# Where two small VectorE instructions of the third batch's routing stand in the queue (clustered attention and mixture of experts on one core)

## The chip, the core and the metric

The kernel runs on one core of one Trainium2 chip, as one program. The metric is the device time of the program in microseconds. Before the change it is 662.63 us, the median of three runs (661.48 to 662.72).

## What is computed

Four batches of 768 tokens with 8 heads of width 64 go through an attention in which a query sees only the keys of its own cluster (the nearest of 16 centroids). The result, 3072 rows of 512, goes through a layer of experts: a row whose skip score is positive is sent to the best of 8 experts, and the expert's answer, times a gate, is added to the row.

```
q_assign = argmax(q_n . c_n);  k_assign = argmax(k_n . c_n)
scores = q k^T / 8, kept where q_assign == k_assign
x = softmax(scores) v                       # 3072 x 512
do_compute = x @ w_skip > 0
e = argmax(x @ w_gate);  g = softmax(x @ w_gate)[e]
out = x;  out[do_compute] += g * (relu(x @ w1[e]) @ w2[e])
```

## The kernel before

**Attention.** Two heads make a pair; four batches of four pairs give 16 pairs, numbered 0 to 15. Each pair is worked in 24 score steps (`NS`). A score step is two matmuls into a PSUM bank `ps` (L604, L605), the exponential on ScalarE into one of twelve slots of `PT` (L607), and an add into a running sum `acc` on GpSimd (L613 for the first add of a half pair, L619 for the others; ten adds to a half pair, and steps 0 and 1 of each half have none). Six steps at a time are multiplied with the values (L630). Beside them run, for the next pair, the 24 maxima: a matmul into a bank (L569) and a row maximum of it into `M` on VectorE (L571). Seven PSUM banks go round among all these; a bank is taken by a matmul again when the instruction that reads it has finished.

**Routing.** When a batch's four pairs are done, its tokens are routed while the next batch's attention runs. `route_slots` (L828) does the second half: each token's rank in its expert's list, one-hots of rank and half, the matmuls that write the lists into `slotacc`, and at its end `route_e` (L983), which keeps for each token a code for the overflow lists. `route_e` begins with `cc` (L989), the product of the token's expert one-hots `ohd` (bf16) and the experts' codes `ecode` (float32), 128x48 with both inputs in SBUF, and `c` (L992), its sum over the experts. Five more small instructions (L995 to L1003) make the code of them.

**The early list.** Behind the third batch (the routing that starts with pair 11, `self.npair - HP - 1`) the list of expert 0 is made ready early: `early_lists` (L1149) counts (L1153), pads (L1156 to L1159), makes the list's row numbers (`slot_ids`, L1195 to L1198) on VectorE, and GpSimd gathers the rows `xe` with an indirect DMA (L1181). The rows are turned by TensorE later (L1172).

**What sets the order.** The order of the attention's instructions is written out by hand: every task has a due time in score steps, counted from its pair's start, and `steps` (L304) takes the tasks in the order of these times and records their instructions. Each engine runs its own in that order. A task that is a generator hands back a pair `(t,)`: go on when the clock stands at `t`. For `route_slots` these times stand in the tuple `SLOTS` (L57): of its 20 entries the last seven are those of `route_e`, 91.67 for `cc`, 91.68 for `c`, and 97.66 to 97.7 for the rest. For the early list the times are 85.4 for the count, 85.67 for padding and row numbers, and 0.2 later for the gather. Counted from pair 11 both lie in pair 14. At 85.8 stands the rest of an expert weight's split on VectorE, `rawW` (L1024).

Of the kernel before, what the change touches and what calls it, by code (L numbers as in the profile page):

```python
# [25 lines left out]
HP = H // 2  # L26
# [29 lines left out]
         53.16, 53.17, 53.18, 61.67, 61.68, 67.67, 67.68, 73.66, 73.67)  # L56
SLOTS = (59.1, 59.11, 59.12, 59.13, 73.7, 73.71, 77.16, 77.17, 77.18, 77.19, 79.66, 82.9, 83.1,  # L57
         91.67, 91.68, 97.66, 97.67, 97.68, 97.69, 97.7)
FIRST = {
    0: {  # L60
        "load_v": -18.9, "sims": -20.0, "hi": (-19.9, -19.8, -19.7, -19.6), "assign": (-19.0, 0.1, 0.01, 0.01, 0.01, 0.01),
# [18 lines left out]
class Kernel:  # L80
# [246 lines left out]
    def tasks(self, i):  # L327

        p, last = {**PLAN, **FIRST.get(i, {})}, i == self.npair - 1
        r = [(s, lambda s=s: self.score(i, s)) for s in range(NS)]  # L330
# [497 lines left out]

    def route_slots(self, i, bt):

        wait = iter([(t,) for t in SLOTS])
        yield from self.route_c(i, bt * KT, KT, wait)
        yield next(wait)
        yield from self.route_cum(KT, wait)
        yield next(wait)
        yield from self.route_d(i, bt * KT, KT, wait=wait)
        yield next(wait)
        yield from self.route_e(i, bt * KT, KT, wait)
# [657 lines left out]
```

## Time and profile before

| | before |
|---|---|
| time, median of 3 runs | 662.63 us (661.48 to 662.72) |
| time of the profiled execution | 662.12 us |
| its span, first to last instruction | 660.4 us |
| TensorE busy | 639.8 us, 97% |
| VectorE busy | 505.6 us, 77% |
| ScalarE busy | 417.3 us, 63% |
| GpSimd busy | 359.9 us, 54% |
| mean granted TensorE clock | 0.989 |

The profile is of one execution. The span leaves out 1.7 us of that execution's own time, at its two ends. PE is TensorE, DVE VectorE, ACT ScalarE and POOL GpSimd; times are counted from the first instruction. A busy share is of the span; "L989" is line 989 of the kernel before. The clock is a share of TensorE's full 2.4 GHz, so 0.50 is its lower level, 1.2 GHz. In the timeline instructions of one kind in a row are put together as "x8", with the first one's start and the time to the last one's end; consecutive instructions of one engine overlap a little in it. In brackets stands the idle time before, and what ended it.

### The profile page before, as it was taken

What the parts mean: (1) busy time and instruction counts of PE and PEld (TensorE: products, weight loads), DVE (VectorE), ACT (ScalarE), POOL (GpSimd) and SP (SyncE); (2) the same over time, 40 slices, a digit from 0 to 9 for tenths busy, and PEclk for the clock granted to TensorE, in tenths of its full rate; (3) what the DMA queues carried; (4) which work ended last, traced back from release to release, by engine and by line L of the source; (5) the groups of instructions that cost most, each with busy time, mean ns of one, the idle gap of its engine ahead of it and who ended that gap; (6) DMA issues with size and microseconds to landing.
All of it is one profiled execution on the core that took longest, in us unless ns stands there. A gap on an engine that the chain in (4) does not pass through costs nothing.

```text
span 660.4 us, 12489 instructions
## 1 busy us (share of the span) xinstructions
PE 639.8 (97%) x4019; PEld 475.9 (72%) x4019; DVE 505.6 (77%) x1031; ACT 417.3 (63%) x935; POOL 359.9 (54%) x384
## 2 busy tenths in 40 slices
PE   7899999999999999999999999799999999999994
PEld 3667776776767767767767767455798898899893
DVE  7877787688988869998769899786689867666721
ACT  7467778677777777767777778454365454544620
POOL 8876777857758867668677777440331321121101
PEclk9899999999999999999999999799999999999998
DMA  7388647866786466555754652140386758566620
GB/s 216 108 198 223 157 140 197 224 184 171 200 224 175 124 168 163 165 137 158 202 145 119 156 136 82 45 151 25 128 283 222 258 189 276 184 199 226 200 77 33
DMA packets 54323, 110.12 MB, mean 167 GB/s; under 512 B 8599, under 2 KB 22807, under 8 KB 54256
## 3 DMA queue, kind: packets, MB, share of 16 engines
q1 hardware_dynamic: 51232, 101.92, 53.7%
q0 software_dynamic: 2624, 7.18, 3.1%
q8 instruction: 33, 0.54, 0.3%
q14 instruction: 34, 0.28, 0.2%
q10 hardware_dynamic: 400, 0.20, 0.1%
HBM read 60.93 MB, written 10.55 MB: 108 GB/s over the span
## 4 chain that ended last, share of the span: by engine, by line
PE 79%; DVE 8%; issue 6%; DMA 5%; ACT 0%; POOL 0%; POOLq 0%; DVEq 0%
PE ps L630 20%; PE ps L604 11%; PE ps L569 10%; PE ps L605 9%; DMA out<-yo,idw 3%; DVE M L571 3%; PE ph L1030 3%; PE ph L1029 3%; PE ph L1028 3%; PE py L1029 2%; PE py L1028 2%; PE py L1030 2%; PE ps L729 2%; PE ps L586 2%; PE ps L480 2%
## 5 line engine op out<-in xcount | busy, mean ns | idle before, releaser
L619 POOL TENSOR_TENSOR acc<-acc,PT 128x384 f32<-128x384 f32 x246 | 241.6, 1010 | 56.5 <-ACT PT L607 56.1
L607 ACT ACTIVATE PT<-ps 128x384 f32<-128x384 f32 x384 | 184.2, 492 | 94.7 <-PE ps L605 77.8
L571 DVE TENSOR_REDUCE M<-ps 128x1 f32<-128x384 f32 x384 | 200.3, 553 | 47.5 <-PE ps L569 46.5
L630 PE MATMUL ps<-PT,vt 128*64 128x385 f32 x768 | 140.2, 500 | 0.1
L604 PE MATMUL ps<-D 98*128 98x384 f32 x384 | 135.5, 353 | 4.1 <-DVE M L571 3.5
L569 PE MATMUL ps<-D 96*128 96x384 f32 x384 | 135.6, 359 | 0.8 <-ACT D L549 0.7
L605 PE MATMUL ps<-D 128*128 128x384 f32 x384 | 131.0, 341 | 0.0
L630 PEld LDWEIGHTS ps<-PT,vt 128*64 128x64 f32 x768 | 49.8, 137 | 57.8 <-issue 52.9
L604 PEld LDWEIGHTS ps<-D 98*128 98x128 f32 x384 | 73.4, 191 | 24.9 <-issue 19.0
L613 POOL TENSOR_TENSOR acc<-PT 128x384 f32<-128x384 f32 x64 | 54.3, 868 | 67.7 <-ACT PT L607 36.1
L569 PEld LDWEIGHTS ps<-D 96*128 96x128 f32 x384 | 73.7, 193 | 20.4 <-ACT x L751 7.2
L1186 POOL DMA_INDIRECT out<-yo,idw x15 | 20.3, 1350 | 114.0 <-DVE yo L1062 103.8
L605 PEld LDWEIGHTS ps<-D 128*128 128x128 f32 x384 | 73.6, 192 | 0.0
L1314 ACT ACTIVATE hh<-ph 128x256 fp32r<-128x256 f32 x56 | 21.4, 383 | 46.4 <-PE ph L1030 46.4
L1315 DVE SCALAR_TENSOR_TENSOR hl<-ph,hh 128x256 fp32r<-128x256 f32 x56 | 23.6, 422 | 33.6 <-ACT hh L1314 33.4
L1286 ACT ACTIVATE D<-wraw 128x1024 fp32r<-128x1024 f32 (+1 forms) x45 | 44.1, 1002 | 6.2 <-PE py L1030 4.7
L1028 PE MATMUL ph<-x2l,D 128*128 128x256 f32 x168 | 47.7, 284 | 0.0
L1029 PE MATMUL ph<-x2h,D 128*128 128x256 f32 x168 | 47.6, 283 | 0.0
L1028 PE MATMUL py<-D,hh 128*128 128x512 f32 x112 | 45.0, 402 | 0.0
L751 ACT ACTIVATE x<-ps,rs 128x64 f32<-128x64 f32 x162 | 36.1, 322 | 10.1 <-DVE rs L683 9.1
L1287 DVE TENSOR_TENSOR D<-wraw,D 128x1024 fp32r<-128x1024 f32 (+1 forms) x29 | 34.3, 1183 | 6.2 <-ACT D L1286 5.4
L431 DVE TENSOR_TENSOR raw<-raw,D 128x768 fp32r<-128x768 f32 x28 | 38.3, 1367 | 0.0
(311 smaller groups left out, 1068.9 us busy)
## 6 DMA issues: line engine op xcount, KB each, us to landing
wraw<-w SPq DMA_DIRECT2D x72, 512.0 KB, 4.9
D<-D SPq DMA_DIRECT2D x124, 192.0 KB, 3.4
raw<-qk SPq DMA_DIRECT2D x16, 768.0 KB, 5.6
D<-raw SPq DMA_DIRECT2D x60, 192.0 KB, 4.1
vt<-v SPq DMA_DIRECT2D x16, 384.0 KB, 4.4
out<-x SPq DMA_DIRECT2D x31, 192.0 KB, 3.3
D<-mk SPq DMA_DIRECT2D x120, 24.0 KB, 1.9
out<-yo,idw POOLq DMA_INDIRECT x15, 4.5
```

Source lines behind the costliest of these rows:

```text
L431: eng.tensor_tensor(out=lo.bitcast(F32R), in0=lo, in1=c[f"hi{t}"].bitcast(F32), op=ALU.subtract)
L569: nc.tensor.matmul(sm, lhsT=c["qm"][a][0:96, j * P:(j + 1) * P], rhs=c["kb"][a][0:96, hf * HALF:(hf + 1) * HALF], start=True, stop=True)
L571: nc.vector.tensor_reduce(out=c["m"][:, j, a, hf:hf + 1], in_=sm, axis=AX.X, op=ALU.max)
L604: nc.tensor.matmul(ps, lhsT=c["kb"][a][0:98, ks], rhs=c["qm"][a][0:98, sl], start=True, stop=False)
L605: nc.tensor.matmul(ps, lhsT=c["kc"][a][:, ks], rhs=c["qc"][a][:, sl], start=False, stop=True)
L607: nc.scalar.activation(out=pt, in_=ps, func=AF.Exp, scale=D ** -0.5)
L613: nc.gpsimd.tensor_tensor(out=acc, in0=self.pt(i, s - 2)[:, :HALF], in1=pt, op=ALU.add)
L619: (nc.vector if dve else nc.gpsimd).tensor_tensor(out=acc, in0=acc, in1=pt, op=ALU.add)
L630: nc.tensor.matmul(av[a * D:(a + 1) * D, :], lhsT=c["vt"][:, kt, a * D:(a + 1) * D], rhs=self.pt(i, hf * 2 * KT + kt * 2 + a), start=(kt = ...
L1028: mm(ps, lhsT=ah, rhs=bl, start=first, stop=False)
L1029: mm(ps, lhsT=ah, rhs=bh, start=False, stop=False)
L1286: nc.scalar.activation(out=h[:, cs], in_=r[:, cs], func=AF.Copy)
```

## The change

In the third batch's routing alone, the times of `cc` and `c` become 85.9 and 85.91, in place of 91.67 and 91.68. All else, and the other batches, stay. The changed kernel has two lines more, so its line numbers behind L57 are higher by one, and behind L829 by two.

```diff
+CODES = {91.67: 85.9, 91.68: 85.91}
...
     def route_slots(self, i, bt):
 
-        wait = iter([(t,) for t in SLOTS])
+        early = i == self.npair - HP - 1
+        wait = iter([(CODES.get(t, t) if early else t,) for t in SLOTS])
         yield from self.route_c(i, bt * KT, KT, wait)
```

The order of TensorE, ScalarE, GpSimd and the DMA queues is the same in both kernels; one place on VectorE differs. VectorE before, in pair 14 behind the row numbers of the early list (`ps_81` and the like are the PSUM banks, `M_200` the maxima, `MX_195` their maximum over a half):

```order
L1024 TENSOR_TENSOR rawW<-wraw,D 128x1024
L571 TENSOR_REDUCE M_200<-ps_81 128x1
L571 TENSOR_REDUCE M_200<-ps_87 128x1
L578 TENSOR_REDUCE MX_195<-M_200 128x3x2
L571 TENSOR_REDUCE M_200<-ps_86 128x1
L571 TENSOR_REDUCE M_200<-ps_82 128x1
L571 TENSOR_REDUCE M_200<-ps_84 128x1
L571 TENSOR_REDUCE M_200<-ps_83 128x1
L571 TENSOR_REDUCE M_200<-ps_85 128x1
L989 TENSOR_TENSOR cc<-ohd,ecode 128x48
L992 TENSOR_REDUCE c_4571<-cc 128x6
L571 TENSOR_REDUCE M_200<-ps_84 128x1
```

Here `cc` and `c` stand behind seven maxima. VectorE in the changed kernel, the same stretch:

```order
L1026 TENSOR_TENSOR rawW<-wraw,D 128x1024
L572 TENSOR_REDUCE M_200<-ps_81 128x1
L991 TENSOR_TENSOR cc<-ohd,ecode 128x48
L994 TENSOR_REDUCE c_4517<-cc 128x6
L572 TENSOR_REDUCE M_200<-ps_87 128x1
L579 TENSOR_REDUCE MX_195<-M_200 128x3x2
L572 TENSOR_REDUCE M_200<-ps_86 128x1
L572 TENSOR_REDUCE M_200<-ps_82 128x1
L572 TENSOR_REDUCE M_200<-ps_84 128x1
L572 TENSOR_REDUCE M_200<-ps_83 128x1
L572 TENSOR_REDUCE M_200<-ps_85 128x1
L572 TENSOR_REDUCE M_200<-ps_84 128x1
```

The two have moved up past six maxima and `MX_195`, and stand behind the first maximum that follows `rawW`. TensorE beside it, from the matmul that fills bank `ps_87` for the second of these maxima to the one that takes the bank again:

```order
L569 MATMUL ps_87<-D 128x384
L604 MATMUL ps_83<-D 128x384
L605 MATMUL ps_83<-D 128x384
L569 MATMUL ps_86<-D 128x384
L604 MATMUL ps_85<-D 128x384
L605 MATMUL ps_85<-D 128x384
L569 MATMUL ps_82<-D 128x384
L604 MATMUL ps_81<-D 128x384
L605 MATMUL ps_81<-D 128x384
L569 MATMUL ps_84<-D 128x384
L604 MATMUL ps_87<-D 128x384
```

Nothing has moved on TensorE: nine matmuls stand between the two uses of `ps_87`, in both kernels.

## Rows read from the trace of the kernel before

**Rows 1.** The page's first line.
```profile
span 660.4 us, 12489 instructions
```

**Rows 2.** TensorE's waits, whole span: waiter, releaser, us in total, times, longest.
```profile
PE ps L604 <- DVE M L571: 3.5, 1, 3.5
```

**Rows 3.** Busy time of each engine in stretches of 4 us, with TensorE's granted clock.
```profile
410.00:414.00 4.00, 4.00 (x25) 2.52 (x23) 4.00 (x3) 3.00 (x8) 4.00 (x6) 1.00 0.18 68
414.00:418.00 4.00, 0.63 (x4) 0.31 (x2) 3.97 (x4) 0.98 (x2) 3.30 (x4) 0.98 0.00 0
418.00:422.00 4.00, 3.88 (x13) 2.96 (x15) 3.56 (x13) 2.30 (x4) 0.00 (x0) 0.50 0.00 0
422.00:426.00 4.00, 4.00 (x16) 1.84 (x13) 1.25 (x2) 1.05 (x4) 0.00 (x0) 0.67 0.59 180
```

**Rows 4.** TensorE's timeline, 408 to 425 us: start, length, instruction, idle before and releaser.
```profile
408.67 0.34 PE L604 MATMUL ps<-D 98*128 98x384 f32 x1
...
409.74 0.49 PE L586 MATMUL ps<-ident,MX 128*128 128x128 f32 x3
410.16 2.16 PE L630 MATMUL ps<-PT,vt 128*64 128x385 f32 x12
412.25 0.44 PE L604 MATMUL ps<-D 98*128 98x384 f32 x1
...
418.12 0.69 PE L604 MATMUL ps<-D 98*128 98x384 f32 x1 [3.49 <-DVE M L571]
...
420.21 0.84 PE L729 MATMUL ps<-ident,oT 128*128 128x128 f32 x3
420.98 3.95 PE L630 MATMUL ps<-PT,vt 128*64 128x385 f32 x12
424.86 0.44 PE L604 MATMUL ps<-D 98*128 98x384 f32 x1
```

**Rows 5.** VectorE's timeline, 407 to 418 us.
```profile
407.75 0.55 DVE L571 TENSOR_REDUCE M<-ps 128x1 f32<-128x384 f32 x1
...
408.29 2.40 DVE L571 TENSOR_REDUCE M<-ps 128x1 f32<-128x384 f32 x5
410.61 6.75 DVE L989 TENSOR_TENSOR cc<-ohd,ecode 128x48 f32<-128x48 bf16 x1
417.40 0.20 DVE L992 TENSOR_REDUCE c<-cc 128x6 f32<-128x48 f32 x1
```

**Rows 6.** GpSimd's timeline, 407 to 424 us.
```profile
407.08 1.38 POOL L1181 DMA_INDIRECT xe<-out,idre  x1 [1.43 <-issue]
408.49 1.68 POOL L613 TENSOR_TENSOR acc<-PT 128x384 f32<-128x384 f32 x2
410.13 7.16 POOL L619 TENSOR_TENSOR acc<-acc,PT 128x384 f32<-128x384 f32 x8
```

**Rows 7.** All `cc` (ns: min/median/max), then the first batch's, and GpSimd beside it.
```profile
L989 DVE TENSOR_TENSOR cc<-ohd,ecode x5: 176/867/6753, 202.1 to 475.9; 128x48 f32<-128x48 bf16 x3, 128x24 f32<-128x24 bf16 x2
...
202.08 0.87 DVE L989 TENSOR_TENSOR cc<-ohd,ecode 128x48 f32<-128x48 bf16 x1
...
199.51 7.92 POOL L619 TENSOR_TENSOR acc<-acc,PT 128x384 f32<-128x384 f32 x8
```

**Rows 8.** Weight splits of the expert stage: group (busy us, mean ns), then one beside a gather.
```profile
L1287 DVE TENSOR_TENSOR D<-wraw,D 128x1024 fp32r<-128x1024 f32 x27 | 32.9, 1220 | 6.2 <-ACT D L1286 5.4
...
515.01 1.22 DVE L1287 TENSOR_TENSOR D<-wraw,vtW 128x1024 fp32r<-128x1024 f32 x1
...
514.43 1.21 POOL L1181 DMA_INDIRECT xg<-out,idr  x1 [0.31 <-PE ph L1030]
```

**Rows 9.** ScalarE's timeline, 407 to 410 us.
```profile
407.16 2.09 ACT L607 ACTIVATE PT<-ps 128x384 f32<-128x384 f32 x4 [0.45 <-ACT rawW L1022]
```

**Rows 10.** The early gather's issue and landing (us); the turn of its rows on TensorE.
```profile
xe<-out,idre POOLq DMA_INDIRECT x1, 4.7
...
426.02 0.60 PE L1172 MATMUL ps<-ident,xe 128*128 128x128 f32 x4
```

## The prediction

> **What bounds the kernel now.** First the page: TensorE is busy 97% of the 660.4 us span [rows 1], so only time that TensorE loses can be won. Then TensorE's waits: the longest by far is one single wait, 3.5 us before a score matmul (L604), ended by a row maximum on VectorE (L571) [rows 2]. Then the stretches around it: from 410 to 414 us TensorE is busy throughout at full clock, from 414 to 418 it works 0.63 us of 4, and then the granted clock is 0.50 for 4 us and 0.67 over the next 4, that is, at the lower level for most of this time [rows 3]. So the wait is paid twice, as idleness and as slow work behind it.
>
> Then the three engines in that window. TensorE idles 3.49 us up to 418.12 [rows 4]. VectorE shows why: it isn't idle, it stands in one instruction, `cc`, from 410.61 for 6.75 us, with the maxima that TensorE's banks wait for queued behind it [rows 5]. GpSimd runs eight adds (L619) without a gap from 410.13 for 7.16 us, to 417.29; `cc` ends 0.07 us later, at 417.36 [rows 5, 6]. The five `cc` take 0.176 us at the least, 0.867 in the middle and 6.753 at the most, and the 0.87 us one also lies in a run of adds, but waited for no more than one add's length (7.92 us for eight is 0.99 each) [rows 7]. I read the 6.75 us as a small VectorE instruction with two SBUF inputs kept out by GpSimd's adds, and here by all that were left of the run, not by one.
>
> What the long hold has of its own isn't plain from the rows. It came into the run with GpSimd late: the gather's wait and the gather (407.08 to 408.46) had put the adds behind, so ten of them followed without a pause [rows 6]. For the forecast it is enough that the hold ended with the run.
>
> **The change, part by part.** No instruction is added or removed; two move on VectorE, no other queue changes.
>
> Removed, the idleness: 3.49 us on TensorE [rows 4]. Its cause is gone from the old place: behind the seventh maximum VectorE goes straight on to the next one.
>
> Removed, the slow work: from 418.12 to 424.86, 6.74 us, TensorE does six score and maximum matmuls, three turns (L729) and twelve L630 [rows 4]. The same kinds at full clock stand just before: six such matmuls from 408.67 to 409.74, 1.07 us; three turns of the same 128x128 size (L586) to 410.16, 0.42; twelve L630 to 412.25, 2.09 [rows 4]. Together 3.58, so 6.74 - 3.58 = 3.16 us come back. By the granted clock it would be 4 x 0.50 + 4 x 0.33 + 4 x 0.02 = 3.4 us [rows 3]; I take 3.16, since it is counted on the very instructions, and keep 3.4 as an end. Sum removed: 6.65 us.
>
> Added at the new place: `cc` would start where the second maximum started, at 407.75 [rows 5]. An unhindered `cc` of 128x48 isn't in the trace; the shortest, half the size, took 0.176 us, so I estimate 0.2, and `c` took 0.20 [rows 5, 7]. The second maximum (bank `ps_87`) then starts 0.4 later and ends at 407.75 + 0.40 + 0.55 = 408.70. TensorE takes that bank again with the L604 at 408.67 [rows 4], so it waits some 0.1 us with the signal's way. The banks behind it keep the same distance, so this is paid once. Ends: 0 and 0.40 us; a gain is excluded, as the maxima only get later. I take 0.1, since 408.70 is next to 408.67. Cover for the rest is VectorE's own slack: no further maximum is due until the L604 at 412.25 and its follower have run [rows 4].
>
> Is `cc` free at 407.75? GpSimd then is in the gather, 0.67 us after its start, and the first add comes at 408.49 [rows 6]: 0.74 us for 0.2 us of work. Beside a gather the trace has a nearer row than any add: a weight split (L1287, two SBUF inputs) that began at 515.01, inside the gather of 514.43 to 515.64, took 1.22 us, which is the mean of its 27 (1220 ns) [rows 8]. So a gather that runs doesn't hold up such an instruction, and I take no wait. The other end is to wait out the gather or more, which are rivals below.
>
> The Trainium skill (SBUF — State Buffer, "Who interferes with whom") says that a VectorE instruction with two SBUF inputs contends with a GpSimd instruction that reads SBUF, and that the second to issue is blocked until the first finishes. On the adds the trace agrees that there is a block, but not on its length: by the rule the hold would have ended with the add under way, at about 411.1 instead of 417.3, and there would have been nothing to win here. Where rule and row differ the row decides.
>
> What is late next: the other small instructions of the code (L995 to L1003) and the next weight split stay behind six more maxima. At full clock these would be over about 416, so their first can still meet the run of adds, which ends at 417.29 [rows 6], and lose up to 1.3 us. No maximum of pair 14 is left behind them, so TensorE doesn't wait for that. The gathered rows land 4.7 us after issue, about 413.2, and are turned at 426.02, in future some 6.6 us earlier, 419.4 [rows 10]: 6 us to spare.
>
> Sum: 662.12 - 3.49 - 3.16 + 0.10 = 655.57; I say **655.5 us**. The profiled execution lies 0.5 us under the median of its three runs (662.63), which is within their scatter.
>
> **The rivals.**
>
> *The gather does block `cc`.* If the gather, which started first, keeps `cc` out until it ends at 408.46, `cc` is 0.71 us later than 407.75 [rows 5, 6]; if it then gets in before the add, the second maximum ends at 409.41, TensorE loses 0.8 us in place of 0.1, and the time is 656.2. Against it speaks the split that ran freely beside a gather [rows 8]. This is the case if `cc` lasts longer than about 0.5 us. The rule of the Trainium skill named above (SBUF — State Buffer, "Who interferes with whom") would make it so, since the gather reads its row numbers from SBUF and was issued first.
>
> *`cc` is held at the new place, by gather and adds* (the slower one). If `cc` hasn't begun when the add starts at 408.49, it waits as before until GpSimd runs dry. TensorE would then stop at 408.67 for want of `ps_87`; by then ScalarE has made four slots of `PT` to add (to 409.25) [rows 9], so GpSimd has four adds: 1.68 us from 408.49, and two of 7.16 / 8 = 0.90, to 411.9 [rows 6]. `cc` ends at 412.0, `c` and the maximum at 412.75, and TensorE idles about 3.95 us, 0.45 more than now. The same work follows at low clock: 662.6. If a second stretch like that of 6.74 us fell to the low level, 3.4 us more: 666.0. The idleness is only an eighth longer than now, so I take a quarter of that way, 663.5. For it: the 6.75 us itself [rows 5]. Against: the 0.74 us that are free of adds [rows 6], and the split beside a gather [rows 8].
>
> *Something later takes part back.* What follows moves forward by 6.6 us, but weight loads and gathers of the expert stage take their time from landings. For it: DMA queues stand still while TensorE does (share 0.00 from 414 to 422 [rows 3]), so the stall may have given them a lead. Against: 6 us to spare at the gather, and TensorE full at 422 to 426. It would cost 1.5 to 5.5 us: 657 to 661.
>
> *No change.* The hold isn't GpSimd's doing, and `cc` or its follower waits the same elsewhere: 662.1. For it: one add was enough in the other batch. Against: the end 0.07 us behind the run's.
>
> **How the numbers follow.** Forecast as reasoned 0.77; gather blocks 0.06; part taken back 0.05; no change 0.06; held at the new place 0.06. The first three are faster by over 0.2% (1.3 us, about what a measurement of this kernel can tell from no change): 0.88. The fourth, and a sixth of the last, whose lower end is within 0.2%, are the same: 0.07. The rest of the last is slower: 0.05. The range starts at 654.5: 662.12 less 3.49 and 3.4, with nothing added, is 655.2, and the shortest of the runs (661.48) lies 0.6 below the profiled one. It ends at 659.0, with the second case and half of the third in it; what is left out above is some 0.15.
>
> **What would show it.** In the new profile `cc` should stand between 407.7 and 408.2, lasting 0.2 us, right behind one maximum and during the gather. GpSimd's ten adds should be as before, to about 417.3, and TensorE should have no wait of over 0.5 us between 406 and 425, at clock 1.00. The turn of `xe` should come at about 419.4, and all behind it 6.5 us earlier than before. It would be wrong if `cc` lasts over 0.5 us (the gather blocks), if VectorE stands in it till about 412 and TensorE idles from 408.8 (held), if another VectorE instruction shows several us in that run of adds, or if the wait is gone and the span isn't shorter by 6 us, when the new waits of the expert stage would name what took it.

## The result, and the profile after

The changed kernel takes **654.36 us** (median of 6 runs, 654.25 to 655.62); the kernel before, run beside it, 661.92 (6 runs, 659.60 to 662.72). The ratio is 0.9897, its 95% interval 0.9876 to 0.9917: 1.0% faster. The forecast was 655.5, in a range from 654.5 to 659.0, so the measured median lies 0.14 us below the range's lower end. The profiled execution took 654.36 us as well.

TensorE's waits in the whole span of the changed kernel (waiter, releaser, us in total, times, longest):

```profile
span 652.6 us, 12489 instructions
...
PE ps L587 <- DVE MX L579: 1.6, 3, 1.2
PE ps L278 <- DVE ones_bf L131: 1.2, 1, 1.2
```

The row of [rows 2], one wait of 3.5 us for a maximum, is gone; what now stands first stood second before. The stretches of [rows 3] in the changed kernel (TensorE's busy time comes first, its granted clock third from the end):

```profile
410.00:414.00 4.00, 4.00 (x24) 3.11 (x21) 1.99 (x4) 2.82 (x6) 3.98 (x5) 1.00 0.00 0
414.00:418.00 4.00, 4.00 (x25) 2.48 (x24) 4.00 (x10) 3.24 (x5) 2.15 (x3) 1.00 0.11 33
418.00:422.00 4.00, 4.00 (x32) 2.01 (x31) 2.77 (x6) 3.19 (x9) 2.64 (x3) 1.00 0.45 154
422.00:426.00 4.00, 4.00 (x26) 2.47 (x25) 3.13 (x7) 2.78 (x6) 0.86 (x1) 1.00 0.29 65
```

TensorE is busy in all 16 us and the clock stays at its upper level, where it stood at 0.50 and 0.67 behind the wait. TensorE's timeline of the changed kernel, for [rows 4]:

```profile
407.28 0.33 PE L570 MATMUL ps<-D 96*128 96x384 f32 x1
407.48 0.44 PE L605 MATMUL ps<-D 98*128 98x384 f32 x1
...
409.08 2.16 PE L631 MATMUL ps<-PT,vt 128*64 128x385 f32 x12
411.18 0.44 PE L605 MATMUL ps<-D 98*128 98x384 f32 x1
...
414.88 2.16 PE L631 MATMUL ps<-PT,vt 128*64 128x385 f32 x12
416.97 0.44 PE L605 MATMUL ps<-D 98*128 98x384 f32 x1
...
418.15 0.60 PE L1174 MATMUL ps<-ident,xe 128*128 128x128 f32 x4
```

From the L604/L605 at 412.25 (now 411.18) to the one at 424.86 (now 416.97) it was 12.61 us and is 5.79. VectorE's timeline of the changed kernel, for [rows 5]:

```profile
406.06 0.55 DVE L572 TENSOR_REDUCE M<-ps 128x1 f32<-128x384 f32 x1
406.53 0.20 DVE L991 TENSOR_TENSOR cc<-ohd,ecode 128x48 f32<-128x48 bf16 x1
406.76 0.20 DVE L994 TENSOR_REDUCE c<-cc 128x6 f32<-128x48 f32 x1
406.88 0.55 DVE L572 TENSOR_REDUCE M<-ps 128x1 f32<-128x384 f32 x1
...
415.13 1.05 DVE L997 CAST ri<-rank 128x6 int32<-128x6 f32 x1
```

GpSimd's timeline of the changed kernel, for [rows 6]:

```profile
405.83 1.40 POOL L1183 DMA_INDIRECT xe<-out,idre  x1 [1.41 <-issue]
407.27 1.68 POOL L614 TENSOR_TENSOR acc<-PT 128x384 f32<-128x384 f32 x2
408.91 7.24 POOL L620 TENSOR_TENSOR acc<-acc,PT 128x384 f32<-128x384 f32 x8
```

`cc` takes 0.20 us beside the gather and ends 0.54 us before the first add starts. The adds are as they were; what meets them now is the small `ri`, which takes 1.05 us, to the last add's end, with nobody waiting for it. All five `cc`, for [rows 7], in ns:

```profile
L991 DVE TENSOR_TENSOR cc<-ohd,ecode x5: 175/198/865, 200.9 to 467.9; 128x48 f32<-128x48 bf16 x3, 128x24 f32<-128x24 bf16 x2
```

The 6.75 us is gone, and the first batch's, held for one add, is now the longest.

Not all of the difference is the change's. The gather starts 1.25 us earlier than before, although nothing ahead of it has moved. The stretches from 20 us on show where that comes from, first in the kernel before:

```profile
20.00:24.00 4.00, 3.46 (x15) 2.88 (x16) 3.81 (x8) 2.88 (x6) 3.86 (x6) 0.73 0.18 69
24.00:28.00 4.00, 4.00 (x23) 3.13 (x23) 2.77 (x6) 2.21 (x5) 3.23 (x4) 0.84 0.13 31
```

and in the changed kernel:

```profile
20.00:24.00 4.00, 3.23 (x20) 2.78 (x19) 3.90 (x8) 3.24 (x7) 3.86 (x6) 1.00 0.19 75
24.00:28.00 4.00, 4.00 (x26) 2.57 (x27) 3.67 (x9) 2.62 (x6) 4.00 (x5) 1.00 0.13 31
```

The execution profiled before had 0.73 and 0.84 of the clock there, the one after 1.00. From 33 us on up to the gather the same maxima start about 1.2 us earlier than before, and that lead stays the same on the way. The clock there goes by the execution, not by the kernel: of the first four variants below, three show 1.00 from 20 to 24 us and one 0.74.

### The profile page after: what moved, and what is told of

Same layout as the page of the kernel before. It is cut to its first block, busy times and chain, and to the rows that moved or that the text cites. A ratio compares the mean times of both kernels' runs of the same rounds, so it can differ in the third digit from the quotient of the medians.

```text
span 652.6 us, 12489 instructions
## 1 busy us (share of the span) xinstructions
PE 635.6 (97%) x4019; PEld 473.0 (72%) x4019; DVE 499.6 (77%) x1031; ACT 417.8 (64%) x935; POOL 360.0 (55%) x384
## 3 DMA queue, kind: packets, MB, share of 16 engines
q0 software_dynamic: 2624, 7.18, 3.2%
## 4 chain that ended last, share of the span: by engine, by line
PE 80%; DVE 7%; issue 6%; DMA 5%; ACT 0%; POOL 0%; POOLq 0%; DVEq 0%
PE ps L631 20%; PE ps L605 11%; PE ps L570 11%; PE ps L606 10%; DMA out<-yo,idw 3%; PE ph L1031 3%; PE ph L1030 3%; PE ph L1032 3%; DVE M L572 3%; PE py L1031 2%; PE py L1030 2%; PE py L1032 2%; PE ps L730 2%; PE ps L587 2%; PE ps L481 2%
## 5 line engine op out<-in xcount | busy, mean ns | idle before, releaser
L631 PE MATMUL ps<-PT,vt 128*64 128x385 f32 x768 | 138.4, 495 | 0.1
L605 PE MATMUL ps<-D 98*128 98x384 f32 x384 | 134.6, 350 | 0.6 <-ACT D L592 0.6
L631 PEld LDWEIGHTS ps<-PT,vt 128*64 128x64 f32 x768 | 49.4, 136 | 56.8 <-issue 52.2
L605 PEld LDWEIGHTS ps<-D 98*128 98x128 f32 x384 | 72.8, 190 | 21.0 <-issue 18.6
```

Of the source, the lines that this page charges most:

```text
L605: nc.tensor.matmul(ps, lhsT=c["kb"][a][0:98, ks], rhs=c["qm"][a][0:98, sl], start=True, stop=False)
L631: nc.tensor.matmul(av[a * D:(a + 1) * D, :], lhsT=c["vt"][:, kt, a * D:(a + 1) * D], rhs=self.pt(i, hf * 2 * KT + kt * 2 + a), start=(kt = ...
```

## The experiments

The forecast rested on a hold whose length it could not explain: GpSimd's adds kept `cc` out for all that were left of the run, while the first batch's `cc` waited for one [rows 7]. So the experiments ask what makes a hold long. Medians of the kernel before, run beside the variants: 660.42 us (13 runs) for the first four, 660.88 (7) for the next four, 661.45 (3) for the three after these, 660.61 (7) for the last.

**A memset among the adds.** The kernel before with

```diff
+        tasks.append((14 * NS + 18.5, 0, self.gap))
...
+    def gap(self):
+        self.nc.gpsimd.memset(self.fix.tile([P, D], F32, name="gap"), 0.0)
```

> The kernel before (cc at its old place), with one small GpSimd instruction more: a fill of a 128x64 tile, which reads nothing, between the fifth and the sixth of the ten adds. Theory (cc is kept out by adds that follow each other without a pause): the fill is the pause, so cc begins at its old place, but ends when the fifth add does, after some 2.2 us in place of 6.75; VectorE goes on before TensorE is out of banks, TensorE has no long wait, and the time is that of the changed kernel, about 6.5 us under the one before. Rival (the hold has another cause, or ends only when TensorE and GpSimd are out of work): 6.7 us as before, and the time of before.

Measured 661.25 us, ratio 1.0007 (0.9994 to 1.0021). VectorE's and GpSimd's timelines of this variant:

```profile
409.43 6.85 DVE L990 TENSOR_TENSOR cc<-ohd,ecode 128x48 f32<-128x48 bf16 x1
...
408.95 2.64 POOL L620 TENSOR_TENSOR acc<-acc,PT 128x384 f32<-128x384 f32 x3
411.54 0.14 POOL L1151 MEMSET gap<- 128x64 f32 x1
411.65 4.56 POOL L620 TENSOR_TENSOR acc<-acc,PT 128x384 f32<-128x384 f32 x5
```

`cc` stands past the memset and ends at 416.28, 0.07 us behind the last add. The theory's 2.2 us didn't come: an instruction that only writes, 0.14 us of it, does not let VectorE in. It is shorter than `cc` itself (0.20 us); a longer one in this place was not tried.

**The gather later.** The kernel before with the gather behind the eighth add instead of ahead of the first:

```diff
-        yield 0.2
-        self.gather(self.xe[:, 0, :], rd, self.ntok - S)
         yield (91.66,)
         self.early = wr, self.slot_gates(acc, const, P, 1, "e")
+        yield (93.5,)
+        self.gather(self.xe[:, 0, :], rd, self.ntok - S)
```

> The kernel before (cc at its old place), with the early gather later by 7.6 score steps, between the eighth and ninth of the ten adds; GpSimd is then not late when the adds begin. Theory (the long hold needs a GpSimd that is behind with its adds): cc still falls into the run of adds, but waits for one add, at most 1.0 us, and the time is 5 to 6.5 us under that of before; the rows land later, which may cost TensorE up to 1 us at their turn. Rival (an instruction with two SBUF inputs that comes into any run of adds by itself is kept out to the end of the run): 5 us or more, and the time of before.

Measured 655.26 us, ratio 0.9916 (0.9891 to 0.9940), with `cc` at its old place: it stands from 409.45 for 0.64 us, one add's rest. So the place alone isn't it; something that comes with the gather ahead of the adds is. This run takes away two things at once, the gather and the lateness of the adds.

**A probe at the old place.** The changed kernel with an instruction of `cc`'s form where `cc` stood:

```diff
+        tasks.append((11 * NS + 91.67, 0, self.probe))
...
+    def probe(self):
+        if not hasattr(self, "prb"):
+            self.prb = self.fix.tile([P, KT, E], F32, name="prb")
+        self.nc.vector.tensor_tensor(out=self.prb, in0=self.ident_bf[:, :KT * E].rearrange("p (j e) -> p j e", e=E),
+                                     in1=self.ecode.unsqueeze(1).to_broadcast([P, KT, E]), op=ALU.mult)
```

> The changed kernel, with an instruction of cc's form (128x48, one bf16 and one float32 input, both in SBUF, no one waits for its result) at cc's old place. Theory (the place decides): it is held for about 6.7 us there, TensorE idles about 3.5 us, and the time is back at that of before. Rival (it was cc's own data or neighbours): 0.2 to 1.0 us, and the time of the changed kernel.

Measured 655.87 us, ratio 0.9922 (0.9895 to 0.9950). Its timelines, VectorE's two rows and then GpSimd's:

```profile
407.72 0.90 DVE L992 TENSOR_TENSOR cc<-ohd,ecode 128x48 f32<-128x48 bf16 x1
...
411.64 2.17 DVE L1155 TENSOR_TENSOR prb<-ident_bf,ecode 128x48 f32<-128x48 bf16 x1
...
407.19 1.24 POOL L1190 DMA_INDIRECT xe<-out,idre  x1 [1.58 <-issue]
...
410.13 3.61 POOL L621 TENSOR_TENSOR acc<-acc,PT 128x384 f32<-128x384 f32 x4
414.42 3.61 POOL L621 TENSOR_TENSOR acc<-acc,PT 128x384 f32<-128x384 f32 x4 [0.68 <-ACT PT L609]
```

The probe is held over the ends of adds, up to 413.74, where GpSimd runs out of `PT`, and ends 0.07 us later: here the run pauses, so TensorE loses nothing by it. That is neither the 6.7 us of the theory nor the rival's 1.0 at most: the place holds the probe, but the run was shorter. And `cc`, at the changed place, took 0.90 us: it came 0.53 us into the gather and got in where that ended (408.43). TensorE then waited 0.58 us for a maximum. So `cc` can be held there until the gather ends.

**A place in between.** The changed kernel with `cc` two maxima (and `MX`) further back:

```diff
-CODES = {91.67: 85.9, 91.68: 85.91}
+CODES = {91.67: 88.0, 91.68: 88.01}
```

> The changed kernel, with cc and c two maxima further back, behind the one of bank ps_86, so that cc comes when the first of the ten adds has just begun. Theory (kept out while adds follow each other): held over several adds, some 3 to 5 us, until TensorE stops for want of banks and GpSimd runs out of adds; TensorE idles 2 to 4 us, and the time is between 3 us under and 1 us over that of before. Rival (kept out for one add): 1.0 us at most, no long wait on TensorE, and a time within 0.5 us of the changed kernel.

Measured 655.49 us, ratio 0.9918 (0.9894 to 0.9942). `cc` came at 407.60 into the first add (407.36), waited for its end and was through in 0.72 us. The theory of a long hold here fell; the rival with one add was right.

**A pause in the run.** The kernel before with four copies on ScalarE ahead of the exponential for the seventh add:

```diff
+        tasks.append((14 * NS + 19.95, 0, self.late))
...
+    def late(self):
+        t = self.fix.tile([P, 3, P], F32, name="late")
+        for _ in range(4):
+            self.nc.scalar.activation(out=t, in_=self.ident.unsqueeze(1).to_broadcast([P, 3, P]), func=AF.Copy)
```

> The kernel before, with four copies of 128x384 on ScalarE put ahead of the exponentials that follow 412.06 us (some 2.2 us of work in a stretch where ScalarE waited 0.91), so that the adds run out of PT: the seventh add, which began at 413.71 with its PT ready only 0.25 us before, can't begin until about 414.8. Theory (the hold lasts over back-to-back adds and ends at the first real pause of GpSimd, here of about 1 us): cc ends within 0.1 us of the sixth add's end, near 413.7, having taken about 3.1 us instead of 6.75; the wait of 3.49 us for a maximum is gone or below 1 us, and the time is 656 to 658.5 (some wait for ScalarE's late exponentials may be new). Rival (cc waits for something else than a pause, a number of adds or the end of the run): cc ends as late as before or later, 417 to 418.5, the wait stays at 3 us or more, and the time is 661.5 or above.

Measured 655.71 us, ratio 0.9925 (0.9900 to 0.9949). VectorE and GpSimd in this variant:

```profile
409.67 3.20 DVE L990 TENSOR_TENSOR cc<-ohd,ecode 128x48 f32<-128x48 bf16 x1
...
415.92 0.76 DVE L996 CAST ri<-rank 128x6 int32<-128x6 f32 x1
...
409.19 3.61 POOL L620 TENSOR_TENSOR acc<-acc,PT 128x384 f32<-128x384 f32 x4
413.99 3.62 POOL L620 TENSOR_TENSOR acc<-acc,PT 128x384 f32<-128x384 f32 x4 [1.20 <-ACT PT L608]
```

The theory was right: `cc` ends at 412.87, 0.07 us behind the add before the pause, and not at the run's end. TensorE then meets no wait over 1.2 us, and making ScalarE's work longer by 2.2 us (the four copies, 2.20 in this trace) made the kernel 5 us faster. Behind the pause the run lets others in: `ri` ends at 416.68, with adds up to 417.61.

**One SBUF input.** The kernel before with the early list's `cc` made by a reduce that copies the one-hots:

```diff
-        vec.tensor_tensor(out=cc, in0=ohd, in1=self.ecode.unsqueeze(1).to_broadcast([P, n, E]), op=ALU.mult)
+        if i == self.npair - HP - 1:
+            vec.tensor_reduce(out=cc, in_=ohd.unsqueeze(3), axis=AX.X, op=ALU.add)
+        else:
+            vec.tensor_tensor(out=cc, in0=ohd, in1=self.ecode.unsqueeze(1).to_broadcast([P, n, E]), op=ALU.mult)
```

> The kernel before with cc of the early list, at its old place behind the seven maxima, made by a reduce over a last dimension of one (it copies the one-hots; the product with the experts' codes is left out there): same output, same place, one SBUF input instead of two. Theory (it is the second SBUF input that GpSimd's adds keep out): the instruction takes 0.2 us at about 410.6 in the middle of the run of adds, no wait of 3.5 us, 655.0 to 656.5. Rival (any small VectorE instruction that comes to that run, or the place by itself): it stands there for 6 us or more and the time is 660 to 662.

Measured 655.69 us, ratio 0.9923 (0.9899 to 0.9947), with this row on VectorE at the old place, in a run of adds as long as before (410.27, 7.18 us, eight):

```profile
410.75 0.19 DVE L990 TENSOR_REDUCE cc<-ohd 128x48 f32<-128x48 bf16 x1
```

With the codes' input gone from SBUF, the instruction isn't held: for `cc` it is the second SBUF input that is kept out. That is what the Trainium skill says too (SBUF — State Buffer, "Who interferes with whom": an instruction with at most one SBUF input doesn't contend, outside the modes that the section calls 2-port); the 0.19 us agree. One input alone is no pass for every kind, though: the cast `ri` has a single SBUF input, and the run's last adds held it for 1.05 us in the changed kernel and for 1.30 in the next variant, where it takes 0.16 elsewhere.

**Further ahead.** The changed kernel with `cc` and `c` ahead of `rawW`:

```diff
-CODES = {91.67: 85.9, 91.68: 85.91}
+CODES = {91.67: 85.75, 91.68: 85.751}
```

> The changed kernel with cc and c moved further up, ahead of the weight split rawW and behind the row numbers, when GpSimd is at its last add of the pair before or idle ahead of the gather. If the changed place still costs what was read off it (0.15 us more distance at TensorE's twelve L631), this gives it back and no more: 0.2 us below the changed kernel at most, 654.2 to 655.5. cc takes 0.2 us, or up to 0.9 where the add of 403.5 is still under way. If the row numbers, the gather or the weights wait for it: 655.5 to 656.5.

Measured 655.74 us, ratio 0.9909 (0.9889 to 0.9929), above the 655.5 that the expectation allowed. `cc` took 0.20 us, but the gather now waited for `c`:

```profile
407.25 1.57 POOL L1183 DMA_INDIRECT xe<-out,idre  x1 [1.62 <-DVE c L994]
```

TensorE's twelve L631 started at 410.36, 1.28 us later than in the changed kernel, and 1.20 of that had been there since the early stretch (0.73 and 0.84 in this execution too). So the 0.15 us were not given back. They are far below the runs' scatter anyway (654.55 to 655.96), and the ratio's interval overlaps the changed kernel's. No variant here beats it.

**Probes elsewhere.** Two probes of `cc`'s form in each of twelve pairs. The expectation calls the base the changed kernel; what ran was the kernel before, with `cc` at its old place:

```diff
+        tasks += [(i * NS + h + i % 6, 0, self.probe) for i in range(1, 13) for h in (5.3, 17.3)]
```

> The changed kernel with 24 instructions of cc's form (128x48, two SBUF inputs, their result unused) put into VectorE's queue, two in each of the pairs 1 to 12. Where a probe comes while GpSimd adds, theory A (held until GpSimd really pauses, however many adds that takes): holds spread up to the length of the runs of adds, several over 2 us, and they end within 0.1 us of the end of a run. Theory B (one add is the rule, and a longer hold needs adds that already wait for GpSimd, as behind a late gather): nearly all holds of 0.2 to 1.0 us; those over 1.1 us only where the next add's PT had been ready for over 1 us. Time 654.5 to 657 by B, above 660 if A makes TensorE wait in several pairs.

660.84 us in one run, 0.04 below the kernel before. The 24 probes as a group (ns: min/median/max), and the early list's `cc` in the same execution:

```profile
L1153 DVE TENSOR_TENSOR prb<-ident_bf,ecode x24: 196/557/1050, 54.3 to 357.4; 128x48 f32<-128x48 bf16 x24
...
409.92 6.76 DVE L990 TENSOR_TENSOR cc<-ohd,ecode 128x48 f32<-128x48 bf16 x1
```

TensorE's single wait for a maximum was 3.5 us here too. In ordinary runs of adds no probe is held beyond about one add, though many come into adds that follow each other without a gap; the `cc` behind the gather is held for 6.76 us. Theory A fell for ordinary runs. What was left was lateness (theory B) or the gather itself.

**Late adds without the gather.** The kernel before, gather moved as above, and in its place

```diff
+        tasks.append((11 * NS + 85.9, 0, self.busy))
...
+    def busy(self):
+        t = self.fix.tile([P, HALF], F32, name="busy")
+        for _ in range(7):
+            self.nc.gpsimd.memset(t, 0.0)
```

> The kernel before with the early gather moved behind the eighth add (as in the run that moved it there), and seven memsets of 128x384 on GpSimd (0.42 us each in its own rows, 2.9 together, from about 404.5) in the gather's old place: the adds start late by about as much as in the kernel before, with no gather ahead of them. cc at its old place. Theory (the backlog makes the long hold: adds whose PT has long been ready follow each other without the pause that would let cc in): cc is held over at least four adds, 3.3 us or more, up to the gather, and TensorE waits again for a maximum; 657 to 662. Rival (the gather itself, ahead of the adds in GpSimd's queue, is what makes the hold long): cc takes one add, 0.2 to 1.0 us, no long wait, 654.5 to 656.5.

Measured 655.38 us (2 runs), ratio 0.9906 (0.9878 to 0.9935). VectorE's `cc`, then GpSimd:

```profile
409.53 0.92 DVE L990 TENSOR_TENSOR cc<-ohd,ecode 128x48 f32<-128x48 bf16 x1
...
404.50 3.27 POOL L1009 MEMSET busy<- 128x384 f32 x7
407.74 1.68 POOL L614 TENSOR_TENSOR acc<-PT 128x384 f32<-128x384 f32 x2
409.38 5.41 POOL L620 TENSOR_TENSOR acc<-acc,PT 128x384 f32<-128x384 f32 x6
```

The adds run back to back and late: they start 0.47 us later than in the changed kernel (407.27), whose early stretch ran at the same clock of 1.00. `cc` comes into the third of them as before, and it is in behind that one. My theory of the lateness fell: it is the gather ahead of the adds that makes the hold long.

**Another moment.** The kernel before with two reduces of 0.2 us ahead of `cc`:

```diff
+        tasks.append((11 * NS + 91.665, 0, self.shift))
...
+    def shift(self):
+        t = self.fix.tile([P, KT], F32, name="shift")
+        for _ in range(2):
+            self.nc.vector.tensor_reduce(out=t, in_=self.ident[:, :KT * E].rearrange("p (j e) -> p j e", e=E),
+                                         axis=AX.X, op=ALU.add)
```

> The kernel before with two small reduces of one SBUF input (0.2 us each) ahead of cc, so that cc comes to the third add 0.4 us later, near its end instead of in its middle. Theory (the state of GpSimd's run decides, not the moment within an add): cc is held to the end of the run as before, 6.3 us, ending within 0.1 us of the last add, with the 3.5 us wait; 660 to 663. Rival (chance of the moment): it gets in at one of the next two ends of an add, 0.2 to 1.1 us, and 654.5 to 656.5.

661.17 us in one run. `cc` stood from 409.76 for 6.50 us, to 0.06 us behind the last add, and TensorE's wait was 3.6 us. The moment within an add isn't it.

**The second add.** The changed kernel with `cc` two maxima behind the place in between:

```diff
-CODES = {91.67: 85.9, 91.68: 85.91}
+CODES = {91.67: 89.5, 91.68: 89.51}
```

> The changed kernel with cc two maxima further back than in the run that held it for one add, so that it comes in the second add of the run behind the gather instead of the first. If the run is open only at its start (the first end of an add), cc is held for several adds, 2 us or more, until the adds really pause (at about 412.5 to 413 in this kernel's timing) or to their end, and TensorE may wait: 656 to 661. If it is open at each end of an add up to there, cc takes 0.2 to 1.0 us: 654.5 to 656.5.

660.55 us in one run, with these rows of VectorE and GpSimd:

```profile
409.64 5.95 DVE L991 TENSOR_TENSOR cc<-ohd,ecode 128x48 f32<-128x48 bf16 x1
...
408.51 1.68 POOL L614 TENSOR_TENSOR acc<-PT 128x384 f32<-128x384 f32 x2
410.15 5.37 POOL L620 TENSOR_TENSOR acc<-acc,PT 128x384 f32<-128x384 f32 x6
```

`cc` came into the second add and was held to the end of the eighth, where GpSimd stopped. TensorE waited 3.0 us for a maximum. So the run behind the gather is open at the end of its first add and, in these runs, then no more until it pauses: 0.24 us into the run `cc` got in after one add, 1.13 us into it it was held for seven, and these 0.9 us decide over some 4.5 us of the span (658.9, less 1.1 that this execution lost before 14 us, against 653.3).

**A pause ahead of the run.** The kernel before, with the four ScalarE copies of above ahead of the run's first exponential (the edit is shown against that variant):

```diff
-        tasks.append((14 * NS + 19.95, 0, self.late))
+        tasks.append((14 * NS + 13.95, 0, self.late))
```

> The kernel before, gather and cc at their old places, with the four copies of 128x384 on ScalarE (2.2 us) put ahead of the first exponential of the run (407.16), so that GpSimd ends the gather at about 408.5 and then stands idle for about 1 us before its first add. Theory (a run of adds that follows a gather without a pause keeps VectorE out, and a pause in between undoes that): cc takes 0.2 to 1.0 us although the gather is ahead of the adds, no wait of 3 us for a maximum, 655 to 657.5 (ScalarE's delay may cost up to 1.5 us). Rival (any run behind a gather is like that until it ends, with a pause at its head or not): cc is held for 2 us or more, to the end of the adds that follow each other, and the time is 658 to 664.

Measured 656.45 us (6 runs), ratio 0.9946 (0.9912 to 0.9980). The profiled execution is the slowest of the six, 658.52: its clock stood at 0.60 and 0.54 in the early stretch, and it comes to this place 3.0 us later than the changed kernel. VectorE's `cc`, then GpSimd:

```profile
413.02 0.72 DVE L990 TENSOR_TENSOR cc<-ohd,ecode 128x48 f32<-128x48 bf16 x1
...
408.85 1.39 POOL L1187 DMA_INDIRECT xe<-out,idre  x1 [1.43 <-issue]
411.04 1.67 POOL L614 TENSOR_TENSOR acc<-PT 128x384 f32<-128x384 f32 x2 [0.81 <-ACT PT L608]
412.69 7.19 POOL L620 TENSOR_TENSOR acc<-acc,PT 128x384 f32<-128x384 f32 x8
```

Gather, ten adds without a break and `cc` in the third of them, all as before; only 0.81 us of idleness stand between the gather and the first add. `cc` is in after one add. The time since the gather isn't what decides: `cc` came 2.78 us behind its end here and got in, the probe at the old place 3.21 us behind it and was held. With the run of the late adds this settles the condition, as far as these runs go, each read from one profiled execution: a run of adds that follows a gather without a pause keeps `cc` out behind its first add; a pause at its head (0.81 us) or inside it (0.68 and 1.20) undoes that.

## Why the prediction was right, and where it was off

*The bound, and the 3.49 us.* Right. The wait is gone, and nothing of the kind took its place.

*The slow work, 3.16 us.* Right, and somewhat small together with the wait: the stretch from 412.25 to 424.86 shrank by 12.61 - 5.79 = 6.82 us where the two terms gave 6.65. The slow work alone was 6.82 - 3.49 = 3.33, between the 3.16 and the granted clock's 3.4. The forecast took its size as fixed, and it isn't: in the execution with the 24 probes, with the same wait of 3.5 us, the last two stretches of [rows 3] read

```profile
418.00:422.00 4.00, 4.00 (x18) 2.01 (x18) 3.85 (x12) 2.87 (x4) 0.00 (x0) 0.58 0.19 53
422.00:426.00 4.00, 4.00 (x32) 2.44 (x30) 0.74 (x2) 2.38 (x7) 2.01 (x3) 0.99 0.41 133
```

with a clock of 0.58 and 0.99 where the kernel before had 0.50 and 0.67. What the wait costs behind it thus goes by the execution too; the two fastest runs of the kernel before (659.60 and 659.72) may be such ones, but have no profile.

*The new place, 0.10 us.* 0.15: the new execution was 407.75 - 406.53 = 1.22 us ahead of the old one on VectorE when `cc` was reached, and 412.25 - 411.18 = 1.07 on TensorE at the L605 behind the twelve L631. One matmul shows it, the L605 at 407.48 (0.44 us where its neighbours take 0.34).

*The sum.* 6.82 - 0.15 = 6.67 us for the change, where 6.55 was said: it gives 655.45 from the old execution's 662.12. The other 1.1 us down to 654.36 are the early stretch at low clock (1.22, less some 0.1 lost again behind 417 us), which lay in the execution that the sum was made against, and which the forecast didn't know as something that comes and goes: the range, which went 0.7 us below 655.2, should have gone down by the whole 1.2. That is the step that was missing. The change itself came out at its 6.67 us for the execution that the sum was made against; the ratio's interval, over all runs, stands for 5.5 to 8.2 us.

*"Is `cc` free at 407.75?"* Right in the profiled execution, 0.20 us. The reason given, that a gather that runs doesn't hold such an instruction, is too wide: in the run with the probe `cc` came 0.17 us sooner after the gather's start and waited for its end. The rival "the gather does block `cc`" has happened there, and its run was not told apart from the others by time (655.87). The wider splits bear the reason out: of the 29 on L1287 in the kernel before, four of them begun inside a gather, none took over 1.23 us. So the 0.20 us of `cc` at this place is in part luck; of the two profiled executions that have it in the gather there, one held it.

*"Kept out by GpSimd's adds, and here by all that were left of the run."* Right as a reading of that run: the pause, the one-input form and the moved gather all end it. But "it came into the run with GpSimd late" pointed at the wrong thing; late adds alone held `cc` for 0.92 us. The cause is the gather directly ahead.

*Held at the new place.* The slower rival's mechanism is real and near: 0.9 us behind the place that let `cc` in after one add, `cc` was held 5.95 us, TensorE waited 3.0 us and most of the gain was gone (660.55, of which 1.1 us were lost before 14 us).

*What is late next.* Right: `ri` met the run's last add and no one waited; the turn of `xe` came at 418.15, where 419.4 was said, which less the 1.22 us of the start is 418.2. Nothing later took more than that 0.1 back: TensorE was 7.89 us ahead at 416.97 and the span is 7.8 shorter.

*The Trainium skill's rule* (SBUF — State Buffer, "Who interferes with whom": the second to issue waits until the first finishes) fits all short holds by adds, 0.64 to 0.92 us, one add each, and not the long ones: 6.75, 6.85, 6.76, 6.50 us over eight adds, 5.95 over seven, 3.20 and 2.17 over four and three up to a pause. The measurement decides: behind a gather, from the second add on, "the first" has to be read as all adds up to the next pause.

## What to carry to other kernels

In this kernel a small VectorE product with two SBUF inputs that came into back-to-back GpSimd adds lost one add at most, but in such a run right behind an indirect gather it could lose the run. So put it ahead of the gather (during it, it got in once and was held once) or behind the run, or replace it by a reduce with one SBUF input (a cast with one input was held). When one small instruction is long in a trace, compare it with its twins and ask what stands ahead of the other engine's run, since the run itself looked the same in both. And take one profiled execution as a sample: find out which of its stretches vary by themselves before setting the end of a range.

## What was not expected

- A gather changes how later adds share with VectorE, until GpSimd pauses: 0.72 us with 0.81 us of idleness between gather and adds, 6.75 without. What it leaves behind, and why the first add's end still lets `cc` in (0.72 us there, 5.95 us one add later), stays open.
- When a running gather holds `cc` is open too: 0.20 us when it came 0.70 us into the gather, 0.90 when it came 0.53 into one.
- Slowing ScalarE by 2.2 us at the right place made the kernel before 5.2 us faster.
- One of the 30 runs of the kernel before that stood beside the experiments took 656.15 us, the others 659.8 to 662.6. It has no profile; perhaps `cc` got in there by itself.
